# One hand-written order of opening steps replaced by another in a fused mLSTM and feed-forward kernel

## The chip, the cores and the metric

The kernel runs on one core of a Trainium2 chip. The metric is the device time of one execution in microseconds (us), the median of several runs.

## The reference

Eight heads and four batches of a gated linear recurrence over 768 tokens (mLSTM), whose output, 3072 tokens of 320 channels, goes through a two-matrix feed-forward with a leaky rectifier.

```python
for t in range(S):                      # q, k, v: (4, 8, 768, 40)
    m_new = maximum(f_gate[:, :, t] + m, i_gate[:, :, t])
    f_stab, i_stab = exp(f_gate[:, :, t] + m - m_new), exp(i_gate[:, :, t] - m_new)
    C = f_stab * C + i_stab * outer(v_t, k_t)
    n = f_stab * n + i_stab * k_t
    y[:, :, t] = sigmoid(o_gate[:, :, t]) * (C @ q_t) / maximum(abs(n @ q_t), 1.0)
x = y as (3072, 320)
h = x @ w_in                            # w_in: (320, 2048)
g = maximum(h, 0) + alpha * minimum(h, 0)
out = g @ w_out                         # w_out: (2048, 320)
```

## The kernel before, in words

The 768 tokens of a batch are cut into 6 chunks of 128, so there are 24 chunks; two chunks make a group of 256 tokens, of which there are 12. A chunk is worked out in parallel form: scores of q and k (tile pS) are multiplied with decays (tile E), and that is multiplied with the values (pH); a running state C carries what came before, and its part is pI. The result xn is gated (og), transposed (p1, p2), split into a high and a low part (XH, XL), and then goes through the feed-forward: eight "up" products a group (ph), a rectifier (g), a split into gh and gl, and eight "down" products (po). Because all products are made of high and low parts, each weight is split too: the raw words are loaded (wi, wr, wo), a copy t is made by ScalarE (`scale`), the lowest bits are joined to it by VectorE (`join`), ScalarE casts it to the high part (`high`: WH, W, OH), and the low part (`low`: WL, W, OL) is the difference of the two, on VectorE, or on GpSimd where the step's name ends in p or P instead of l or L. Where a weight's step x is replaced by y, ScalarE's preparation of the lowest bits (`three`, L865) is left out and VectorE does a shift more (`shift`, L871) before the join (L879 instead of L877).

Nothing is scheduled by a planner when the kernel is built. The table ORDER names some 400 steps of the opening (the first batch's six chunks, the splitting of the weights, and the first two groups' feed-forward), and each name is one call; after it PATTERN repeats for the later groups. The program `pin`s that order: on each engine instructions run in the order in which the steps stand, and waits for other engines' results are added. All loads but two are issued by SyncE (SP) in the same order, so a load whose buffer is still read holds back all loads behind it.

Names of steps that matter below: `kfz` clears the two buffers kf (four memsets on GpSimd, L311 and L312), `li0` is GpSimd's subtraction that the first biases need (g_li, L1215), `bj0` is VectorE's that reads it (L1218). `wd` scales the keys (kd, L172), on GpSimd if the chunk's number is in KDP. `um` and `uc` make the next state: if the chunk is in CP, the decayed old state is one GpSimd instruction of 104 partitions (the multiply at L210), else two on VectorE (L221, one for each parity of the heads); VectorE then adds the new product (L222). `gx` is the multiply that writes xn, on GpSimd if the chunk is in XNP. A feed-forward up product has five steps: with U, R, S, G, K the low part gl is on VectorE, with V, r, s, g, N it is on GpSimd (L785). `psa` hands out the four PSUM banks of one pool, two with tag a and two with tag b, in turns.

Of the kernel before, what the change touches and what calls it, by code (L numbers as in the profile page):

```python
# [17 lines left out]
def kernel(ctx: ExitStack, tc: tile.TileContext, q, k, v, i_gate, f_gate, o_gate, w_in, w_out, alpha, out):  # L18
# [19 lines left out]
    ps_o = ctx.enter_context(tc.tile_pool(name="ps_o", bufs=1, space=bass.MemoryType.PSUM))  # L38
    ps_a = ctx.enter_context(tc.tile_pool(name="ps_a", bufs=2, space=bass.MemoryType.PSUM))
    turns = ["b", "a"]  # L40

    def psa(name, tag=None):
        if tag is None:
            turns.reverse()
            tag = turns[0]
        return ps_a.tile([P, 512], F32, tag=tag, name=name)
# [61 lines left out]
    def by_token_of(n, j):  # L108

        t = (qn_t, kn_t)[j][n % NQ]  # L110
        if n < NDIR:
            return t[:, :, :D]
        return t.rearrange("p h e -> p (h e)")[:, : H * D].rearrange("p (h e) -> p h e", e=D)
# [54 lines left out]
    def weighed(n):  # L168

        b, c = divmod(n, NC)  # L170
        kd = sb.tile([P, H, D], F32, tag="kd", name=f"kd{n}")
        (nc.gpsimd if n in KDP else nc.vector).tensor_tensor(  # L172
            kd, by_token_of(n, 1), wT[:, c, b * H : (b + 1) * H].unsqueeze(2).broadcast_to([P, H, D]), ALU.mult
# [8 lines left out]
    def update_steps(n):  # L182
# [8 lines left out]
        if not late or j == 0 or n - 1 not in pus:  # L191
            pu = psa(f"pu{n}", kept(n, "a", NDIR + 1))
            if late and j == 0:
                pus[n] = pu
        else:
            pu = pus.pop(n - 1)
# [11 lines left out]
        old, new = C_t[(n - 1) % 3], C_t[n % 3]  # L208
        if c > 0 and n in CP:
            nc.gpsimd.tensor_tensor(  # L210
                new[:R], old[:R], gamB[:R, b * H : (b + 1) * H, c : c + 1].broadcast_to([R, H, VA]), ALU.mult
            )
        for par in range(2):
# [4 lines left out]
            else:  # L218
                if n not in CP:
                    gam = gamB[r, b * H + par : (b + 1) * H : 2, c : c + 1].broadcast_to([D, NPR, VA])  # L220
# [111 lines left out]
    def values(n, E):  # L332

        pH = psa(f"pH{n}")
        va = va_t[n // GC % NV][:, n % GC]
        for h in range(H):
            nc.tensor.matmul(
                repeated(pH, h * VA, VA), E[h % 2][:, h // 2 * P : (h // 2 + 1) * P],
                va[:, h].unsqueeze(1).broadcast_to([P, WIDE // VA, VA]), start=True, stop=True,
            )  # L340
        return pH[:, : H * VA].rearrange("p (h e) -> p h e", e=VA)
# [27 lines left out]
    def values_by_parts(n, Es):  # L369

        V = vbs.pop(n)
        S = sb.tile([P, H, VA], F32, tag="T", name=f"S{n}")
        for par in range(2):
            pH = psa(f"pH{n}_{par}", kept(n, "a", NDIR))
            for p in range(NPR):
                for k, e in enumerate(Es[par]):
                    nc.tensor.matmul(  # L377
                        pH[:, p * 3 * VA : (p * 3 + 3 - k) * VA], e[:, p * P : (p + 1) * P],
                        V[:, 2 * p + par, : 3 - k], start=k == 0, stop=k == 2,
                    )  # L380
            yield
            nc.vector.tensor_reduce(
                by_parity(S, par), pH[:, : NPR * 3 * VA].rearrange("p (r k e) -> p r e k", k=3, e=VA),
                mybir.AxisListType.X, ALU.add,
            )
            yield S
# [29 lines left out]
    def gated_steps(n, hv):  # L416
# [23 lines left out]
        else:  # L440
            nc.gpsimd.tensor_tensor(sg, sg, rb, ALU.mult)
        yield
        (nc.gpsimd if c > 0 and n in XNP else nc.vector).tensor_tensor(
            xn[:, :DM].rearrange("p (h d) -> p h d", d=D), hv[:, :, :D], sg, ALU.mult
# [211 lines left out]
    def first_stacks():  # L656
# [20 lines left out]
    NBF = 6  # L677
    GF = NDIR // GC
    BEHIND = 4
    XNP = range(2, NBF)  # L680
    KDP = range(1, 24)
    CP = range(6, 24)
    OBA = range(0)
    WIDE = 3 * VA
    ORDER = """warm18 kfz alT lf0z warm2 warm2 i00d i00s sca0 lf0a lf0b dq0 L0 sp01 qT0 dq1 alC li0 bj0 wt0 bTt kT0 i00x qc0 kc0 ewj
        i01d sca1 bTc ex01 sp00 sc00 qT1 wTt eeL wTc qc1 wd0 li1 lf1a lf1b kT1 sc01 i00j ex00 kc1 eTt Cz eTc sp11 ex11
        dv0 wg01 i01s wd1 L1 um0 uc0 i01x lpa um1 sp10 wg00 gma gmd ex10 i01j i00h fm1 ft1 sc11 do0 sc10 wg10 bj1 wtl
        blt ewl blc i00p o0d o0s r0d o0x gmm gmc r0s r0x v0 wg11 lpb lpc lpd uc1 dq2 qT2 o2d gr0 wlt og1 warm2 wlc r0j
        i11d lpe o0j i01h i01p gg0 qc2 dq3 gx0 gp0 kT2 v1 eel elt elc sp21 kc2 sc21 dL r0H ta1 gr1 gg1 sp20 ex21 qT3
        wg21 i10d dv1 r0h gx1 gp1 r0p r0L ex20 wd2 sc20 wg20 qc3 x0 x1 xa0 xd0 dq4 fm2 wd3 xa1 xd1 i10s F0 ft2 o2s o2y  # L690
        sp31 o0h ex31 kT3 o2j o2h i10y i10j um2 U00 o0l V01 kc3 R00 i11s uc2 i11y i11j o2l do1 i10h i10l sp30 r01 qT4
        qc4 ex30 S00 v2 sc31 i20d i20s ta2 gr2 i20x wg31 o1d og2 gg2 gx2 kT4 i20j kc4 sc30 wg30 G00 K00 i21d fm3 ft3
        s01 i20h o1s i20p i11h i11p o1x r2d o1j i21s i21x sc41 v3 um3 i21j uc3 ta3 dL4 U02 V03 r2s r2y o3d gr3 sc40
        ex41 fm4 R02 dq5 o1h o1l o4d g01 r2j N01 qT5 i21h i21p o3s S02 o3x G02 K02 dL5 wg41 i31d ft4 D00 wd4 dq6 o3j
        qc5 dv2 r2h r2p r03 ex40 o4s r2H D01 o4x gg3 s03 o3h o4j gx3 o5d gp3 wg40 i30d V04 r04 s04 dv3 o4h V05 gp2 x2
        x3 xa2 xd2 o6d do2 wd6 kT5 g04 r2P g03 o3l xa3 r05 o4l s05 v4 xd3 kc5 i31s ta4 N03 N04 i31y i31j i30s o5s o5x
        F1 V10 gr4 r10 um4 uc4 dL6 i30x um6 U11 ex50 R11 o5j s10 uc6 S11 ex51 g10 i31h dL7 i31p sc50 N10 i30j dq7 wg50
        U12 fm5 ft5 o5h sc51 wg51 v5 o7d R12 S12 ta5 D10 G11 K11 o6s o6x gr5 og3 gg5 G12 gx5 gg4 D11 K12 D12 i30h i30l
        gx4 U13 gp5 D02 tp0 do3 U06 o7s gp4 o5l o6j vp0 R13 tp1 g05 S13 G13 N05 K13 o7x o6h D13 vp1 o7j U07 tp2 tp3
        R06 S06 R07 x4 x5 xa5 xd5 D03 D04 D05 S07 o7h o7l G06 K06 o6l D06 xa4 xd4 G07 K07 D07 Z0"""  # L700
    PATTERN = """og.-1 ua.0 uA.1 m1.0 V4<< tf.1 ub.0 vb.1 xn.-1 xp.-1 V5<< tg.1 g2<< m0.0 N2<< vc.1 c1.0 r4<< vb.0 d1.0 th.1 h1.0 ti.1 xw.-1 uc.0
        s4<< ud.0 D2<< ue.0 U6<< g4<< l1.0 g3<< N3<< uf.0 r5<< c0.0 vd.1 vc.0 ua.1 sh.1 X:-1 lG.-1 lG.2 ub.1 s5<< N4<<
        R6<< d0.0 g5<< ug.0 h0.0 l0.0 uc.1 V7<< N5<< vd.0 D3<< D4<< D5<< S6<< ta.2 tb.2 xa:-1 uh.0 lL.2
# [8 lines left out]
    def in_full():  # L712

        names = ORDER.split()
        done = set(names)
# [651 lines left out]
```

## Time and profile before

| what | value |
|---|---|
| median of 3 runs | 465.33 us (464.62 to 466.82) |
| the profiled execution, its own time | 465.35 us |
| its span, first to last instruction | 463.6 us |
| TensorE busy | 452.8 us, 98% |
| VectorE, ScalarE, GpSimd busy | 329.8, 315.0, 308.4 us |

The profiled execution is as long as the median run. Its time is 1.75 us over its span, which lies around the instructions. The engines are called PE (TensorE), DVE (VectorE), ACT (ScalarE), POOL (GpSimd) and SP in the rows; PEld is TensorE's loading of weights. TensorE's granted clock was full in all of the stretches shown.

### The profile page before, as it was taken

Reading aid. Unit: us, or ns where it says so; the run is one execution under the profiler, and the core shown is the slowest. Engines: PE = TensorE matmul, PEld = TensorE weight load, DVE = VectorE, ACT = ScalarE, POOL = GpSimd, SP = SyncE. Lnnn points to the kernel's source line nnn. Section 1 sums busy time; section 2 is a strip of 40 time slices with the busy share of each in tenths; the row PEclk is TensorE's granted clock in tenths of the full one; section 3 lists DMA queues with packets and bytes.
Section 4 is the critical chain, followed back from the end, with each engine's and each line's share of the span. In section 5 each row is a group of like instructions: output and inputs, shape, how many; then the busy total and the mean of one; then the engine's idle time right before and its main releaser. Section 6 shows DMA issues by size and latency. Waiting matters only on the chain.

```text
span 463.6 us, 11813 instructions
## 1 busy us (share of the span) xinstructions
PE 452.8 (98%) x4366; PEld 442.0 (95%) x4366; DVE 329.8 (71%) x692; ACT 315.0 (68%) x707; POOL 308.4 (67%) x377
## 2 busy tenths in 40 slices
PE   8989989999999999999999999999999999999996
PEld 6879978999999999999999999999999999999996
DVE  4989998747776787886875887886776786764321
ACT  4899898676857858758856958757857858423331
POOL 8551674854698697588888598588888686324231
PEclk9999999999999999999999999999999999999999
DMA  9999994869775775888997686688796463020000
GB/s 184 177 221 252 277 252 118 175 122 190 151 182 147 138 184 160 137 174 173 158 187 176 122 197 168 133 166 180 153 206 156 107 154 90 1 84 15 28 2 28
DMA packets 186306, 68.67 MB, mean 148 GB/s; under 512 B 150234, under 2 KB 178506, under 8 KB 186250
## 3 DMA queue, kind: packets, MB, share of 16 engines
q1 hardware_dynamic: 186170, 67.83, 67.2%
q8 instruction: 34, 0.56, 0.5%
q14 instruction: 22, 0.18, 0.2%
q10 hardware_dynamic: 80, 0.11, 0.1%
HBM read 40.44 MB, written 7.57 MB: 104 GB/s over the span
## 4 chain that ended last, share of the span: by engine, by line
PE 83%; DVE 5%; DMA 5%; SPq 3%; ACT 3%; issue 1%; ACTq 0%; DVEq 0%
PE po L796 36%; PE ph L759 5%; PE ph L765 5%; PE ph L762 5%; PE ph L760 5%; PE ph L761 5%; PE ph L764 4%; PE ph L763 4%; PE ph L766 4%; PE pH L377 4%; PE pS L515 4%; DMA wi<-in_moe_w_in_dram 2%; DMA wr<-in_moe_w_in_dram 2%; PE pI L403 1%; PE pu L203 1%; DMA qn<-in_q_dram 1%
## 5 line engine op out<-in xcount | busy, mean ns | idle before, releaser
L785 POOL TENSOR_TENSOR gl<-g,gh 128x512 fp32r<-128x512 f32 x77 | 100.5, 1306 | 42.9 <-ACT gh L783 39.6
L796 PE MATMUL po<-OH,gh 128*128 128x320 f32 x368 | 110.7, 312 | 0.0
L796 PE MATMUL po<-OL,gh 128*128 128x320 f32 x368 | 109.3, 309 | 0.0
L769 ACT ACTIVATE g<-ph 128x512 f32<-128x512 f32 x96 | 57.1, 596 | 58.2 <-PE ph L766 56.0
L774 DVE SCALAR_TENSOR_TENSOR g<-g,oma,ph 128x256 f32<-128x256 f32 x156 | 66.8, 469 | 32.7 <-ACT g L769 32.3
L796 PEld LDWEIGHTS po<-OL,gh 128*128 128x128 f32 x368 | 69.2, 188 | 0.1
L796 PEld LDWEIGHTS po<-OH,gh 128*128 128x128 f32 x368 | 69.1, 188 | 0.0
L796 PE MATMUL po<-OH,gl 128*128 128x320 f32 x368 | 69.0, 309 | 0.0
L759 PE MATMUL ph<-XH,WH 128*128 128x256 f32 x192 | 57.2, 298 | 1.1 <-ACT wo L865 0.7
L796 PEld LDWEIGHTS po<-OH,gl 128*128 128x128 f32 x368 | 57.9, 188 | 0.0
L764 PE MATMUL ph<-XL,WH 128*128 128x256 f32 x192 | 54.3, 283 | 0.9 <-DVE XL L623 0.9
L765 PE MATMUL ph<-XL,WH 128*128 128x256 f32 x192 | 54.3, 283 | 0.0
L762 PE MATMUL ph<-XH,WL 128*128 128x256 f32 x192 | 54.3, 283 | 0.0
L760 PE MATMUL ph<-XH,WH 128*128 128x256 f32 x192 | 54.1, 282 | 0.0
L761 PE MATMUL ph<-XH,WL 128*128 128x256 f32 x192 | 54.1, 282 | 0.0
L364 ACT CAST E<-pS 128x512 bf16<-128x512 f32 x72 | 41.6, 582 | 18.0 <-DVE pS L361 14.0
L763 PE MATMUL ph<-XH,W 128*128 128x256 f32 x192 | 53.4, 278 | 0.2 <-POOL W L891 0.2
L766 PE MATMUL ph<-XL,W 128*128 128x256 f32 x192 | 53.4, 278 | 0.0
L783 ACT CAST gh<-g 128x512 fp32r<-128x512 f32 x77 | 46.5, 618 | 9.1 <-DVE g L774 6.6
L486 ACT ACTIVATE E<-Lb,bT 128x128 f32<-128x128 f32 x160 | 50.0, 392 | 0.0
L361 DVE TENSOR_TENSOR pS<-pS,E 128x512 f32<-128x512 f32 x36 | 24.8, 690 | 29.6 <-PE pS L515 26.2
L759 PEld LDWEIGHTS ph<-XH,WH 128*128 128x128 f32 x192 | 36.1, 188 | 2.0 <-ACT wo L865 0.9
(197 smaller groups left out, 1123.2 us busy)
## 6 DMA issues: line engine op xcount, KB each, us to landing
Lb<-L_d SPq DMA_DIRECT2D x20, 512.0 KB
wo<-in_moe_w_out_dram SPq DMA_DIRECT2D x8, 640.0 KB
wi<-in_moe_w_in_dram SPq DMA_DIRECT2D x8, 512.0 KB
qn<-in_q_dram SPq DMA_DIRECT2D x24, 160.0 KB
kn<-in_k_dram SPq DMA_DIRECT2D x24, 160.0 KB
va<-in_v_dram SPq DMA_DIRECT2D x24, 160.0 KB
og<-in_o_gate_dram SPq DMA_DIRECT2D x24, 160.0 KB
out_dram<-ob SPq DMA_DIRECT2D x11, 320.0 KB
```

Of the source, the lines that this page charges most:

```text
L759: nc.tensor.matmul(dst, WH[half][:, 0, hs], XH[:, 0], start=True, stop=False)
L760: nc.tensor.matmul(dst, WH[half][:, 1, hs], XH[:, 1], start=False, stop=False)
L761: nc.tensor.matmul(dst, WL[half][:, 0, hs], XH[:, 0], start=False, stop=False)
L762: nc.tensor.matmul(dst, WL[half][:, 1, hs], XH[:, 1], start=False, stop=False)
L763: nc.tensor.matmul(dst, W2[:, fs], X2, start=False, stop=False)
L764: nc.tensor.matmul(dst, WH[half][:, 0, hs], XL[:, 0], start=False, stop=False)
L765: nc.tensor.matmul(dst, WH[half][:, 1, hs], XL[:, 1], start=False, stop=False)
L766: nc.tensor.matmul(dst, W2[:, fs], X2L, start=False, stop=True)
L769: nc.scalar.activation(gt, ph, AF.Relu, scale=-1.0)
L774: nc.vector.scalar_tensor_tensor(out=y[:, e], in0=gt[:, e], scalar=oma[:, f : f + 1], in1=ph[:, e], op0=ALU.mult, op1=ALU.add)
L785: (nc.vector if split else nc.gpsimd).tensor_tensor(gl, y, gh.bitcast(F32), ALU.subtract)
L796: nc.tensor.matmul(po[j], x[:, e, j * P : (j + 1) * P], W[f // NB][:, f % NB], **ends)
```

## The change

The same steps stand in another order. Some change their kind: eight low parts of weights change engine, seven of them from VectorE to GpSimd (o0, o1, o2, o4, o7 and i10 from l to p, and one half of a remainder, r0L to r0P), and one the other way (i00p to i00l); two weights take the step y in place of x (i01, o4); one up product takes the VectorE form (V04 to U04). Three sets of chunks change: keys of chunk 4 go to VectorE (chunk 5 ends the batch and has none), the decayed states of chunks 1 to 4 go to GpSimd, and xn of chunk 1 goes to GpSimd and that of chunk 4 to VectorE. The first 51 PSUM banks that `psa` hands out follow a written list of tags instead of taking turns. The count of warming products stays at 24. PATTERN is unchanged.

```diff
     turns = ["b", "a"]
+    first_turns = list("abababaababaababababaababaababababaabbaabbaabaaabaa")
 
     def psa(name, tag=None):
+        if tag is None and first_turns:
+            tag = first_turns.pop(0)
         if tag is None:
...
-    XNP = range(2, NBF)
-    KDP = range(1, 24)
-    CP = range(6, 24)
+    XNP = (1, 2, 3, 5)
+    KDP = (1, 2, 3, *range(6, 24))
+    CP = (1, 2, 3, 4, *range(6, 24))
...
-    ORDER = """warm18 kfz alT lf0z warm2 warm2 i00d i00s sca0 lf0a lf0b dq0 L0 sp01 qT0 dq1 alC li0 bj0 wt0 bTt kT0 i00x qc0 kc0 ewj
+    ORDER = """sca0 i00d dq0 warm18 lf0a i01d alT li0 i00s i00x lf0b warm3 dq1 lf0z warm2 kfz dv0 L0 bj0 sp01 qT0 alC bTt
```

First place, GpSimd's queue at the start of the program. Before, from the last small memset on (g_li is the subtraction of `li0`, kf the buffers of `kfz`):

```order
L1002 MEMSET unit 32x1
L311 MEMSET kf_133 40x512
L312 MEMSET kf_133 64x512
L311 MEMSET kf_134 40x512
L312 MEMSET kf_134 64x512
L1215 TENSOR_TENSOR g_li<-g_WH_96,g_WL_97 32x256
L1014 TENSOR_TENSOR g_WL_97<-g_WH_96,g_L 32x256
```

After (all lines of the changed file are three to four lines further down):

```order
L1006 MEMSET unit 32x1
L1219 TENSOR_TENSOR g_li<-g_WH_96,g_WL_97 32x256
L314 MEMSET kf_133 40x512
L315 MEMSET kf_133 64x512
L314 MEMSET kf_134 40x512
L315 MEMSET kf_134 64x512
L1018 TENSOR_TENSOR g_WL_97<-g_WH_96,g_L 32x256
```

The subtraction moved ahead of the four memsets.

Second place, VectorE's queue around the third chunk's state (C_87) and the first low parts of the out weights (OL). Before:

```order
L879 SCALAR_TENSOR_TENSOR t_wi_0_538<-wi_0_487,t_wi_0_538 128x512
L891 TENSOR_TENSOR OL_105<-t_wo_362,OH_104 128x640
L221 TENSOR_TENSOR C_87<-C_86,gamB 40x4x42
L222 TENSOR_TENSOR C_87<-C_87,pu_568 40x4x42
L221 TENSOR_TENSOR C_87<-C_86,gamB 40x4x42
L222 TENSOR_TENSOR C_87<-C_87,pu_568 40x4x42
L871 TENSOR_SCALAR t_wi_1_616<-t_wi_1_616 128x512
L879 SCALAR_TENSOR_TENSOR t_wi_1_616<-wi_1_415,t_wi_1_616 128x512
L891 TENSOR_TENSOR OL_564<-t_wo_542,OH_563 128x640
L891 TENSOR_TENSOR WL_103<-t_wi_0_538,WH_102 128x512
```

After:

```order
L883 SCALAR_TENSOR_TENSOR t_wi_0_579<-wi_0_473,t_wi_0_579 128x512
L411 TENSOR_TENSOR T_609<-pI_541,eT 128x336
L225 TENSOR_TENSOR C_87<-C_87,pu_590 40x4x42 x2
L778 SCALAR_TENSOR_TENSOR ph_0_562<-g_0_581,oma,ph_0_562 128x256 x2
L1238 TENSOR_TENSOR T_609<-T_609,pH_600 128x336
L875 TENSOR_SCALAR t_wi_1_611<-t_wi_1_611 128x512
```

Two low parts of 128x640, one of 128x512 and both multiplies with gamB left VectorE's queue there.

Third place, GpSimd's queue from the third chunk's keys on (kd). Before:

```order
L891 TENSOR_TENSOR W_73<-t_wr_371,W_73 64x512
L172 TENSOR_TENSOR kd_501<-kn_77,wT 128x320
L172 TENSOR_TENSOR kd_532<-kn_78,wT 128x320
L443 TENSOR_TENSOR xn_670<-T_540,og_341 128x320
L891 TENSOR_TENSOR WL_711<-t_wi_0_667,WH_710 128x512
L891 TENSOR_TENSOR WL_103<-t_wi_1_616,WH_102 128x512
```

After:

```order
L175 TENSOR_TENSOR kd_445<-kn_77,wT 128x320
L453 COPY xn_389<-xn_389 128x64
L895 TENSOR_TENSOR WL_103<-t_wi_1_320,WH_102 128x512
L446 TENSOR_TENSOR xn_456<-T_341,og_327 128x320
L453 COPY xn_456<-xn_456 128x64
L175 TENSOR_TENSOR kd_502<-kn_78,wT 128x320
L895 TENSOR_TENSOR W_73<-t_wr_397,W_73 64x512 x2
L895 TENSOR_TENSOR OL_105<-t_wo_345,OH_104 128x640
L213 TENSOR_TENSOR C_87<-C_86,gamB 104x336
L895 TENSOR_TENSOR OL_584<-t_wo_504,OH_583 128x640
L895 TENSOR_TENSOR WL_103<-t_wi_0_579,WH_102 128x512
```

The third chunk's keys stand ahead of a weight's low part and of the remainder's (W) now, and both low parts OL, the second half of W and the state's multiply were added.

## Rows read from the trace of the kernel before

**Rows 1.** Stretches: length, busy us (instructions) by engine, TensorE's clock, DMA share, GB/s.

```profile
0.00:12.00 12.00, 9.76 (x66) 7.59 (x66) 4.82 (x14) 6.19 (x13) 10.39 (x28) 1.00 1.02 183
12.00:46.00 34.00, 31.89 (x306) 28.91 (x305) 31.28 (x65) 30.85 (x75) 13.34 (x17) 1.00 0.97 218
46.00:78.50 32.50, 29.60 (x273) 28.17 (x273) 29.00 (x57) 28.17 (x60) 19.82 (x21) 1.00 0.85 213
78.50:460.00 381.50, 381.50 (x3724) 377.36 (x3724) 264.70 (x557) 249.41 (x562) 264.89 (x314) 1.00 0.63 136
```

**Rows 2.** TensorE's waits, 0 to 80 us: us in total, times, longest.

```profile
PE ph L764 <- DVE XL L623: 0.9, 1, 0.9
PE pb L100 <- DVE xn L443: 0.8, 1, 0.8
PE pH L337 <- DVE E L1101: 0.8, 2, 0.6
PE ph L759 <- ACT wo L865: 0.7, 1, 0.7
PE ps_gw L1022 <- ACT E L1080: 0.5, 1, 0.5
PE ph L759 <- DVE g L774: 0.4, 1, 0.4
...
PEld pH L337 <- DVE E L1101: 1.2, 2, 0.8
```

**Rows 3.** The chain that ended last, 46 to 80 us: start, us, what.

```profile
60.39 0.80 ACT wo L865
...
69.17 0.69 DVE t_wi L879
...
71.54 0.83 DVE t_wo L877
```

**Rows 4.** Timeline, 25.8 to 29.2 us, GpSimd and VectorE.

```profile
25.86 1.26 POOL L891 TENSOR_TENSOR WL<-t_wi,WH 128x512 fp32r<-128x512 f32 x1 [0.55 <-ACT WH L887]
25.92 1.55 DVE L439 SCALAR_TENSOR_TENSOR og<-og,r 128x320 f32<-128x320 f32 x1
...
29.09 0.49 DVE L439 SCALAR_TENSOR_TENSOR og<-og,r 128x320 f32<-128x320 f32 x1
```

**Rows 5.** VectorE's groups, 0 to 80 us: busy us, mean ns, idle before.

```profile
L877 DVE SCALAR_TENSOR_TENSOR t_wo<-t_wo,wo 128x640 uint32<-128x640 uint32 x5 | 5.7, 1140 | 0.4 <-ACT wo L865 0.2 <-POOL xn L443 0.2
L877 DVE SCALAR_TENSOR_TENSOR t_wi<-t_wi,wi 128x512 uint32<-128x512 uint32 x5 | 4.6, 923 | 0.0
L891 DVE TENSOR_TENSOR OL<-t_wo,OH 128x640 fp32r<-128x640 f32 x5 | 4.0, 810 | 0.0
L439 DVE SCALAR_TENSOR_TENSOR og<-og,r 128x320 f32<-128x320 f32 x4 | 3.4, 861 | 0.0
L221 DVE TENSOR_TENSOR C<-C,gamB 40x168 f32<-40x168 f32 x8 | 2.5, 318 | 0.1
L879 DVE SCALAR_TENSOR_TENSOR t_wr<-wr,t_wr 128x512 uint32<-128x512 uint32 x1 | 1.8, 1769 | 0.0
L871 DVE TENSOR_SCALAR t_wo<-t_wo 128x640 uint32<-128x640 uint32 x1 | 0.5, 494 | 0.4 <-ACT t_wo L855 0.4
```

**Rows 6.** GpSimd's groups, 0 to 80 us, and C over the whole span.

```profile
L891 POOL TENSOR_TENSOR W<-t_wr,W 64x512 fp32r<-64x512 f32 x3 | 3.8, 1277 | 1.0 <-ACT W L887 0.8
L172 POOL TENSOR_TENSOR kd<-kn,wT 128x320 f32<-128x320 f32 x5 | 3.5, 719 | 0.1
...
L230 POOL TENSOR_TENSOR C<-C,gamB 40x336 f32<-40x336 f32 x12 | 9.0, 753 | 0.0
```

**Rows 7.** SyncE's longest wait total, 0 to 80 us, and the stretch around it.

```profile
SPq L106 <- POOL kd L172: 7.4, 2, 4.1
...
32.00:36.00 4.00, 3.67 (x43) 3.18 (x44) 3.33 (x8) 3.61 (x10) 2.71 (x4) 1.00 0.37 55
```

**Rows 8.** Timeline of the start, VectorE.

```profile
6.68 0.41 DVE L1218 TENSOR_TENSOR g_WH<-g_li,g_L 32x256 f32<-32x256 f32 x1 [0.42 <-POOL g_li L1215]
```

More of the change, by code (lines that the diff above doesn't have):

```diff
@@ L679 @@
     BEHIND = 4
-    XNP = range(2, NBF)
-    KDP = range(1, 24)
-    CP = range(6, 24)
+    XNP = (1, 2, 3, 5)
+    KDP = (1, 2, 3, *range(6, 24))
+    CP = (1, 2, 3, 4, *range(6, 24))
     OBA = range(0)
     WIDE = 3 * VA
-    ORDER = """warm18 kfz alT lf0z warm2 warm2 i00d i00s sca0 lf0a lf0b dq0 L0 sp01 qT0 dq1 alC li0 bj0 wt0 bTt kT0 i00x qc0 kc0 ewj
[L686 to L700, printed above, removed]
@@ new lines @@
+    ORDER = """sca0 i00d dq0 warm18 lf0a i01d alT li0 i00s i00x lf0b warm3 dq1 lf0z warm2 kfz dv0 L0 bj0 sp01 qT0 alC bTt
+        bTc qc0 wt0 ewj kT0 kc0 sp00 wTt ex01 sc00 sca1 i00j wTc wd0 qT1 Cz li1 sp11 kT1 sc01 eeL ex00 wg00 lf1a
+        wg01 eTt qc1 lf1b kc1 L1 eTc um0 uc0 sc11 ex11 wd1 sp10 fm1 sc10 i01s i01y lpa o0d do0 gma gmd i00h ex10
+        i01j ft1 bj1 wtl o0s og1 warm1 ewl um1 wg11 wg10 i00l lpb blt gmm gmc o0x r0d dq2 v0 lpc lpd blc gr0 uc1 r0s
+        r0x eel i01h i11d o2d wlt wlc dq3 lpe gg0 kT2 r0j gx0 qT2 v1 qc2 sp21 wd2 kc2 ta1 elt gp0 gr1 i01p dL sp20
+        elc r0H dv1 o0j i10d r0h dq4 sc21 qT3 gg1 gx1 ex21 wg21 gp1 ex20 wd3 o2s qc3 sc20 wg20 x0 x1 xa0 kT3 r0P r0p
+        i20d xd0 xa1 xd1 fm2 sp31 kc3 F0 o0h o2y o2j ex31 U00 i10s R00 o2h i10y i10j do1 um2 o0p v2 ft2 i11s sp30
+        uc2 i10h o2p V01 S00 o1d i20s qT4 ta2 dL4 i11y kT4 sc31 gr2 ex30 i20x i11j fm3 qc4 i21d r2d i20j dq5 i10p
+        og2 kc4 i11h o1s wg31 ft3 i20h sc30 gg2 i11p wg30 G00 K00 gx2 r01 s01 i20p wd4 o1x sc41 i21s i21x o1j i21j
+        v3 ta3 um3 uc3 U02 gr3 ex41 R02 V03 D00 sc40 r2s r2y fm4 S02 o1h o1p r03 g01 r2j o3d i21h o3s N01 i21p G02
+        o3x r2h r2p o4d dv2 i31d K02 dq6 qT5 dL5 o3j ft4 ex40 o5d r2H D01 dv3 s03 o4s U04 i30d do2 wg41 o4y qc5 R04
+        gg3 kT5 V05 o3h kc5 gp2 gx3 wg40 o4j S04 gp3 x2 x3 wd6 o3l r05 xa2 G04 o4h v4 xd2 xa3 r2P g03 o4p i31s N03
+        K04 xd3 s05 ta4 i31y gr4 o5s o5x i31j F1 V10 um4 uc4 ex51 r10 o6d ex50 um6 U11 R11 i30s dL6 uc6 sc51 sc50
+        s10 o5j i30x i31h g10 wg51 U12 dL7 wg50 S11 fm5 N10 i31p i30j G11 ft5 o7d R12 v5 S12 ta5 o5h D10 i30h og3
+        dq7 K11 gr5 gg5 G12 K12 o6s D11 gg4 gx5 o6x D12 U13 tp0 i30l gx4 D02 o6j R13 vp0 o5l g05 do3 o7s gp5 S13 U06
+        N05 G13 gp4 o7x K13 o6h D13 tp1 U07 o7j tp2 R06 x4 R07 x5 tp3 S06 vp1 D03 xa5 xd5 xa4 o6l D04 G06 S07 o7h
+        D05 K06 G07 o7p D06 xd4 K07 D07 Z0"""
```

## The prediction

> **What bounds the kernel now.** I read the stretches first [rows 1]. From 78.5 us to 460 us TensorE is busy in every microsecond (381.50 of 381.50), so nothing that VectorE, ScalarE, GpSimd or a load does there can shorten it, and the diff leaves that part's order alone. Only the opening, up to 78.5 us, has room: TensorE is idle there for 12.00 - 9.76 = 2.24, 34.00 - 31.89 = 2.11 and 32.50 - 29.60 = 2.90 us, 7.25 us in all. Some of this is the program's start and can't go. A microsecond taken out of the opening should be a microsecond of the end, since the dense part only slides forward.
>
> Second, TensorE's waits in the opening [rows 2]. Four of them end with VectorE: 0.9 for the low part XL, 0.8 for xn (the next product wants the bank that xn still reads), 0.8 for the decayed scores E, 0.4 for the rectified g; 2.9 us together. ScalarE ends 0.7 and 0.5. Matmul ends are modelled, so the true waits are somewhat longer: for E the weight loads show 1.2 where the matmuls show 0.8.
>
> Third, the chain of waits [rows 3] and what VectorE does on it. VectorE is busy for 29.00 of the 32.50 us before 78.5 us, ScalarE for 28.17, GpSimd for 19.82 [rows 1]; from 12 to 46 us it is 31.28, 30.85 and 13.34 of 34. VectorE and ScalarE are nearly full, GpSimd has 34.00 - 13.34 + 32.50 - 19.82 = 33.3 us free.
>
> Fourth, whether VectorE's instructions cost what they should. At 25.92 us the multiply of og takes 1.55 us; at 29.09 us the same takes 0.49 [rows 4]. During the first GpSimd makes a weight's low part, from 25.86 us for 1.26 us; the difference, 1.06 us, is about what was left of that when og came up (1.20). The group's means say the same of others [rows 5]: og 861 ns over four, the joins of t_wo 1140 against 0.83 us alone and of t_wi 923 against 0.69 alone [rows 3], that of t_wr 1769 against 0.69 for the same size. So blocked time on VectorE up to 80 us is 4 x 0.37 + 5 x 0.31 + 5 x 0.23 + 1.08 = 5.3 us.
>
> The Trainium skill ("SBUF — State Buffer", Who interferes with whom) gives the rule: a VectorE instruction with two SBUF inputs contends with a GpSimd instruction that reads SBUF, and the loser waits for the whole of the other; one with a PSUM input doesn't. The rows above agree for og. By the rule alone moving work to GpSimd makes more blockers, which is the rival "lock" below, priced there from rows.
>
> **The change part by part.** *Taken from VectorE* ahead of the last wait (at 78 us): four low parts of 128x640 at 0.81 (3.24), half a remainder, in width like a join without a block (0.69), eight multiplies of C at 0.318 (2.54) [rows 5]; i10 and i00 swap. That is 6.5 us. *Given to VectorE:* one keys' product, which I price like og unblocked, the same size (0.49) [rows 4], one low part gl of 128x512 (0.69, as t_wi alone [rows 3]), two shifts (0.49 and at most 0.49) [rows 5]: 2.2 us. Net -4.3 us. xn of chunk 1 and of chunk 4 change places: nothing.
>
> *Given to GpSimd* [rows 6]: half a remainder 1.28; four low parts of 128x640, which no row has on GpSimd. Between 1.28 (width doesn't count) and 1.28 x 640/512 = 1.60 I take 1.60, since its time follows the row's length (320 long 0.72, 512 long 1.28): 6.4. Four C multiplies of 104 partitions: 0.75 by the row of 40 partitions, 1.95 if partitions counted; I take 0.75, because the remainder's 64 partitions cost 1.28 as do 128 in [rows 4]: 3.0. Taken off it: keys 0.72, one gl 1.28. Net +8.7 us, into 33.3 us free. If the upper price held for C, +13.5, which still fits.
>
> *Taken from ScalarE:* two preparations of lowest bits, at 0.80 for 128x640 [rows 3] and at most that for 128x512: 1.5 us at most.
>
> *SyncE's queue.* SyncE waited 7.4 us for keys, in two waits [rows 7]: the loads of the next chunk's k may not overwrite kn until kd has read it, and every load issued later stood behind. After the first of them the DMA engines were busy only 0.37 of 32 to 36 us, 2.5 us of lost transfer time. In the new GpSimd queue the third chunk's keys stand ahead of a weight's and the remainder's low parts, so that wait should nearly go. TensorE's shown waits for loads are small, so I count it at nothing here; if the loads set the pace it is worth up to 2.5 us (a rival).
>
> *The start.* bj0 waited 0.42 us for li0 [rows 8], which stood behind four memsets in GpSimd's queue; now it stands ahead, so the first biases come 0.4 us earlier. The memsets end later, but the first scores that need kf come several products after.
>
> *Other moves* (warming products, PSUM tags, the places of loads) I count at nothing: the shown wait for a bank is the 0.5 behind ScalarE [rows 2], so they may give back 0.5 or take about as much.
>
> *Sum.* VectorE loses 4.3 us of work and, if the order keeps its two-input instructions clear of GpSimd's, part of 5.3 us of blocking. I take half of that, 2.6, so 6.9 us less on a queue that had 6.2 us idle in 66.5 (12 to 78.5 us). That is more than the 2.9 us of TensorE's waits on it, so I let all four go: 2.9, plus 0.9 for the modelled ends (0.2 to 0.4 each, as the E row shows), plus 0.4 at the start: 4.2. With VectorE out of the way ScalarE, as full as it, will end waits that don't show now: I give back a quarter, 1.0 (chosen; the trace bounds it between nothing and all). Net -3.2 us against the profiled execution's 465.35, which lies at the median: **462.1 us**. Bounds: all idle but the first 2.24 gone and 1.4 for modelled ends, 465.35 - 6.4 = 458.9; everything given back and nothing won, 465.4.
>
> **The rivals.** *ScalarE sets the pace.* It is busy for 30.85 of 34 and 28.17 of 32.5 us [rows 1], and the change takes at most 1.5 us from it; the waits behind ScalarE stay and VectorE's turn into waits for casts. Then the gain is 1.5: 463.9 us. For it: the two engines are equal within 0.9 us in both stretches. Against: four of the six larger waits end with VectorE.
>
> *Loads set the pace.* DMA share is 0.97 in the middle stretch. If TensorE's pace there follows the loads, only the gap at 32 to 36 us is won, 2.5 us: 462.9 us. Against: no long wait of TensorE ends with a load.
>
> *The lock, slower.* GpSimd's reading of SBUF grows by 8.7 us, a quarter of the 33.2 us it was busy from 12 to 78.5 us. VectorE's instructions with two SBUF inputs ahead of the last wait fall from 49 to 35 (counted in the two orders). At the same chance of meeting, blocking would be 5.3 x 35/49 x 1.26 = 4.8 us, so VectorE still gains 4.8. It decides where each of the 35 waits over (5.3 + 4.3)/35 = 0.27 us on average, against 0.11 now. The new low parts of 1.60 us could do that: if every second of the 35 met one and waited half of it, blocking would be 14 us, VectorE 4.4 us later, and TensorE, which would wait for it in full, ends at 469.7 us. Against: the order was moved around on both engines at once and the meetings can be placed; for: a meeting hangs on a few tenths of a microsecond, and ScalarE's and the loads' times shift them.
>
> **How the numbers follow.** Chances: forecast 0.45, loads 0.13, ScalarE 0.28, lock 0.14. Half a per cent, 2.3 us, is about what a measurement of this kernel can tell from no change, so faster means under 463.0. The forecast's spread (459 to 463.5) and the loads make 0.58 faster; ScalarE's case and the edges of the forecast 0.28 same, with what is left of the lock's milder end; slower 0.14. The range goes from the bound of the full gain, 458.9, to 466.0, past ScalarE's case and the mild end of the lock.
>
> **What would show it.** Right: og, t_wo, t_wi and t_wr nearer to their unblocked times in the opening, VectorE's busy time up to the last wait down by 6 us or so, the rows "ph behind XL", "pH behind E" and "pb behind xn" gone or halved, GpSimd fuller by 9 us, the last idle of TensorE at about 75 us and from there an unchanged dense part of 381.5 us. SyncE's long wait for kd shorter, with no gap at 32 to 36 us. Wrong: the same sum of TensorE idle with ScalarE or GpSimd named as releaser, or VectorE instructions with two SBUF inputs at 1.5 us and more behind low parts of 128x640, or new idle in the dense part, should the later groups' loads or parts come late for a TensorE that arrives earlier.

## The result and the profile after

The changed kernel takes 461.02 us (median of 4 runs, 460.83 to 461.09) where the kernel before took 464.98 (median of 4, 464.43 to 466.82): a ratio of 0.9911, 95% interval 0.9892 to 0.9931, 4.0 us less. The profiled execution took 460.83 us, its span is 459.1 us (463.6 before).

The stretches of the changed kernel (columns as in [rows 1]; the last row is the stretch of [rows 7]):

```profile
0.00:12.00 12.00, 10.09 (x69) 8.08 (x70) 7.12 (x17) 6.34 (x15) 9.59 (x30) 1.00 0.94 183
12.00:46.00 34.00, 32.82 (x313) 29.92 (x313) 28.33 (x56) 31.30 (x73) 22.75 (x22) 1.00 1.09 238
46.00:74.00 28.00, 27.54 (x263) 26.63 (x262) 26.20 (x52) 25.55 (x56) 21.94 (x21) 1.00 0.86 221
74.00:455.50 381.50, 381.46 (x3725) 377.33 (x3725) 259.56 (x559) 249.85 (x563) 265.17 (x314) 1.00 0.63 136
...
32.00:36.00 4.00, 3.34 (x39) 2.72 (x37) 3.10 (x5) 3.66 (x9) 3.85 (x4) 1.00 0.97 216
```

The opening now ends at 74 us and not at 78.5, which is 4.5 us earlier; the two profiled executions are 465.35 - 460.83 = 4.5 us apart too, 0.5 more than the medians. TensorE's idle time in it is 1.91 + 1.18 + 0.46 = 3.55 us instead of 7.25, so 3.7 of the 4.5 us are idle time that went; the rest, 0.8, is shorter busy time. This split belongs to the one trace: in the trace of *changed_again*, the same kernel (below), the opening ends at 74.6 us with 3.06 us of idle time, so idle time there is 4.2 us less and busy time 0.3 more. The dense part is as long as it was, 381.46 of 381.50. VectorE's busy time up to the dense part fell from 65.1 us [rows 1] to 7.12 + 28.33 + 26.20 = 61.65; GpSimd's rose from 43.55 to 54.28.

TensorE's waits, 0 to 80 us (columns as in [rows 2]):

```profile
PE ph L767 <- POOL W L895: 0.8, 2, 0.6
PE pb L1056 <- DVE g_L L1157: 0.5, 1, 0.5
PE pqk L269 <- DVE C L225: 0.5, 1, 0.5
```

All six waits of [rows 2] are gone, those on ScalarE too. What is listed now beside the wait for the program's first constants is 1.8 us in three rows, one of them behind GpSimd. The row for g_L is missing in the trace of *changed_again*; the other two stand there as well.

VectorE's groups of the changed kernel, 0 to 80 us (columns as in [rows 5]; its line numbers are three or four higher):

```profile
L881 DVE SCALAR_TENSOR_TENSOR t_wo<-t_wo,wo 128x640 uint32<-128x640 uint32 x4 | 4.5, 1129 | 0.1
...
L883 DVE SCALAR_TENSOR_TENSOR t_wi<-wi,t_wi 128x512 uint32<-128x512 uint32 x4 | 3.1, 771 | 0.0
...
L442 DVE SCALAR_TENSOR_TENSOR og<-og,r 128x320 f32<-128x320 f32 x6 | 3.0, 507 | 0.1
L883 DVE SCALAR_TENSOR_TENSOR t_wo<-wo,t_wo 128x640 uint32<-128x640 uint32 x2 | 2.8, 1419 | 0.0
```

GpSimd's groups of the same stretch:

```profile
L895 POOL TENSOR_TENSOR OL<-t_wo,OH 128x640 fp32r<-128x640 f32 x4 | 7.1, 1772 | 1.9 <-ACT OH L891 1.1 <-DVE gl L789 0.6
L895 POOL TENSOR_TENSOR W<-t_wr,W 64x512 fp32r<-64x512 f32 x4 | 6.6, 1643 | 0.3
L213 POOL TENSOR_TENSOR C<-C,gamB 104x336 f32<-104x336 f32 x4 | 3.7, 923 | 2.1 <-DVE gamB L1194 2.1
```

og, 861 ns in [rows 5], is at 507, nearly unblocked. The joins of t_wo are not: 1129 after 1140, and 1419 for the two that follow a shift. GpSimd's own instructions became longer too: W 1643 on average after 1277 [rows 6].

To have one number for this I add up, from the timelines up to 80 us, how much VectorE's joins, low parts, og and keys (24 to 29 instructions, as records are missing) took over their shortest durations: 0.68 us for 512 columns, 0.82 for 640, 0.48 for 320. That is **5.4 us before and 4.5 after**; the shifts, over 0.42 us (0.49 for 640), add 0.5 before and 1.8 after. Together 5.9 and 6.3. I call it blocked time below, as "joins and so on + shifts".

### The profile page after: what moved, and what is told of

It is laid out like the page before. It is cut to its first block, busy times and chain, and to the rows that moved or that the text cites. A ratio compares the mean times of both kernels' runs of the same rounds, so it can differ in the third digit from the quotient of the medians.

```text
span 459.1 us, 11805 instructions
## 1 busy us (share of the span) xinstructions
PE 452.4 (99%) x4366; PEld 442.2 (96%) x4366; DVE 321.2 (70%) x682; ACT 313.5 (68%) x705; POOL 319.4 (70%) x385
## 4 chain that ended last, share of the span: by engine, by line
PE 91%; DMA 2%; ACT 2%; POOL 2%; DVE 2%; issue 1%; DVEq 0%; ACTq 0%; POOLq 0%
PE po L800 36%; PE ph L763 6%; PE ph L769 5%; PE ph L766 5%; PE ph L768 5%; PE ph L764 5%; PE ph L765 5%; PE ph L767 5%; PE ph L770 5%; PE pH L380 4%; PE pS L518 4%; PE pu L206 2%; PE pS L1101 1%; DMA wo<-in_moe_w_out_dram 1%; PE pI L406 1%; PE pH L340 1%
## 5 line engine op out<-in xcount | busy, mean ns | idle before, releaser
L789 POOL TENSOR_TENSOR gl<-g,gh 128x512 fp32r<-128x512 f32 x76 | 98.6, 1299 | 40.0 <-ACT gh L787 36.9
L767 PEld LDWEIGHTS ph<-XH,W 128*128 128x128 f32 x192 | 36.7, 191 | 1.2 <-POOL W L895 1.2
```

The source lines that it names most:

```text
L767: nc.tensor.matmul(dst, W2[:, fs], X2, start=False, stop=False)
L789: (nc.vector if split else nc.gpsimd).tensor_tensor(gl, y, gh.bitcast(F32), ALU.subtract)
```

## The experiments

Each was timed against the kernel before on the same chip (medians 464.99, 464.49 and 464.84 in three sessions), so kernels of different sessions are compared by their ratios; 0.1% is 0.46 us.

### The order by itself, the engines by themselves

*order_alone*: the new order and list of banks, with each step's old form and the old sets.

```diff
-    XNP = (1, 2, 3, 5)
-    KDP = (1, 2, 3, *range(6, 24))
-    CP = (1, 2, 3, 4, *range(6, 24))
+    XNP = range(2, NBF)
+    KDP = range(1, 24)
+    CP = range(6, 24)
...
-    i01y i00l r0P o0p o2p i10p o1p o4y U04 R04 S04 G04 o4p K04 o7p
+    i01x i00p r0L o0l o2l i10l o1l o4x V04 r04 s04 g04 o4l N04 o7l
```

> The new order and the list of bank tags, but every step on the engine and in the form that it had before (low parts, keys, states, xn, the two joins, the fifth up product). If the moved work is what counts (VectorE has its 4.3 us back, in an order that left no room for it), most of the 4.0 us is lost: 463.5 to 465.5 us. If the order alone made the gain, 461.7 us or less. VectorE's busy time up to TensorE's last wait should be some 4 us above that of the changed kernel in the first case.

*engines_alone*: the reverse, the old order without the list, with the new forms in their old places and the new sets.

> The old order, with the new engines and forms. If the moved work is what counts, 462 to 463.5 us: VectorE is 4.3 us shorter and its four waits shrink. If the order made the gain, no change or worse, 464.5 to 466.5 us, since low parts of 1.6 us on GpSimd meet VectorE's instructions with two SBUF inputs where the old order put them.

Measured: order_alone 467.18 us, ratio 1.0043 (1.0028 to 1.0057); engines_alone 465.78, 1.0016 (1.0005 to 1.0027). Neither half gives anything; each by itself costs, 2.2 and 0.8 us, and both together give 4.0. order_alone came out above both of the ranges that I had expected. In it TensorE's longer waits end with VectorE, but for one behind GpSimd's W (its waits up to 80 us):

```profile
PE pS L1100 <- DVE C L225: 1.5, 1, 1.5
...
PE pb L103 <- DVE XL L626: 1.3, 1, 1.3
PE ph L766 <- POOL W L894: 1.1, 1, 1.1
PE pS L1100 <- DVE T L1237: 1.0, 1, 1.0
PE pqk L269 <- DVE C L225: 1.0, 1, 1.0
```

GpSimd waits for work, and this is its longest wait there:

```profile
POOL WL L894 <- ACT WH L890: 14.9, 1, 14.9
```

I read it so: the order is made for a VectorE that doesn't do the moved work. With that work on VectorE its busy time up to the dense part (which begins at 80.5 us here) is 65.00 us, 3.4 more than the changed kernel's 61.65; GpSimd stands 14.9 us at one low part, and states (C), XL and T come late. SyncE's wait for kd [rows 7] has no row here, and the DMA engines are 0.89 and 1.04 busy in the two halves of 32 to 36 us, so this kernel has the loads' gap closed and is slower all the same.

In engines_alone three of TensorE's four waits for VectorE stay (up to 80 us; the one for XL is gone), that for g is three times as long as in [rows 2], and two behind ScalarE have come, for kf and E (L1080):

```profile
PE ph L759 <- ACT kf L323: 1.2, 1, 1.2
PE ph L759 <- DVE g L774: 1.2, 1, 1.2
PE pb L100 <- DVE xn L443: 0.9, 1, 0.9
PE pH L337 <- DVE E L1101: 0.8, 2, 0.6
PE pqk L266 <- ACT E L1080: 0.8, 1, 0.8
```

Its timeline from 35 to 43 us shows where VectorE's time went; GpSimd's rows, then VectorE's:

```profile
35.54 2.15 POOL L891 TENSOR_TENSOR OL<-t_wo,OH 128x640 fp32r<-128x640 f32 x1 [0.49 <-ACT OH L887]
37.66 0.94 POOL L210 TENSOR_TENSOR C<-C,gamB 104x336 f32<-104x336 f32 x1
38.56 1.55 POOL L891 TENSOR_TENSOR OL<-t_wo,OH 128x640 fp32r<-128x640 f32 x1
...
36.18 1.80 DVE L871 TENSOR_SCALAR t_wi<-t_wi 128x512 uint32<-128x512 uint32 x1
38.01 2.65 DVE L879 SCALAR_TENSOR_TENSOR t_wi<-wi,t_wi 128x512 uint32<-128x512 uint32 x1
```

A shift of 0.42 us takes 1.80, a join of 0.68 takes 2.65, and they end 0.3 and 0.55 us after one of GpSimd's 128x640 subtractions has ended (at 37.69 and 40.11). The join had come up 0.55 us before the second of these began, during GpSimd's multiply of C, and stood until both were over. Blocked time is 9.4 + 2.5 us against 5.4 + 0.5 before: 6.0 us more, over the 4.3 us of work that left VectorE. This is the rival "lock" of the prediction, in the old order.

### Is it GpSimd's reading?

In both orders GpSimd's low parts of weights read only 8 columns (16 for OL) and fill the time with two memsets, which write SBUF and read none of it; beyond those columns the low parts are left zero. In the old order a low part takes GpSimd as long as in engines_alone: WL 2 x 0.516 + 0.248 = 1.28 us (1.32 there), OL 2 x 0.641 + 0.495 = 1.78 (1.70). In the new order, where GpSimd had been held up itself, it is shorter than in the changed kernel: OL 1.55 us (1.77), W 1.51 (1.64).

```diff
-            (engine or nc.vector).tensor_tensor(l, t, h.bitcast(F32), ALU.subtract)
+            if engine is None:
+                nc.vector.tensor_tensor(l, t, h.bitcast(F32), ALU.subtract)
+                return
+            engine.tensor_tensor(l[..., :8], t[..., :8], h[..., :8].bitcast(F32), ALU.subtract)
+            for _ in range(2):
+                engine.memset(l[..., 8:].bitcast(F32), 0.0)
```

> The kernel of engines_alone, where GpSimd's low parts of weights read only 8 columns and then fill the rest by two memsets each, so that GpSimd works for as long but hardly reads SBUF (the low parts themselves are left out: those are zero). If the lock on reading is what ate the gain of the moved work (10.4 us of VectorE's time over its unblocked times there), VectorE's blocked time should fall below 5 us and the time to 462 to 463.5 us. If the lock isn't the cause, within 0.7 us of engines_alone, 465.8.

> The changed kernel with the same replacement. It has 6.0 us of blocked time on VectorE, but TensorE's waits are short: if the new order has put the blocked time where it doesn't count, 460.3 to 461.0 us; if blocked time still counts in full, 458.5 us.

Measured: in the old order 462.14 us, ratio 0.9944 (0.9932 to 0.9957), against 1.0016 for engines_alone: 0.72%, 3.3 us. In the new order 459.33, 0.9885 (0.9870 to 0.9901), against 0.9911: 0.26%, 1.2 us, between the two cases expected. Blocked time fell from 9.4 + 2.5 to 1.1 + 2.1 us in the old order and from 4.5 + 1.8 to 2.5 + 1.2 in the new. The old order's timeline, GpSimd and then VectorE:

```profile
35.10 1.46 POOL L896 MEMSET OL<- 128x624 f32 x2
...
39.04 1.09 POOL L896 MEMSET WL<- 128x504 f32 x2
...
35.00 1.00 DVE L871 TENSOR_SCALAR t_wi<-t_wi 128x512 uint32<-128x512 uint32 x1
36.03 0.69 DVE L879 SCALAR_TENSOR_TENSOR t_wi<-wi,t_wi 128x512 uint32<-128x512 uint32 x1
...
39.07 0.69 DVE L879 SCALAR_TENSOR_TENSOR t_wi<-wi,t_wi 128x512 uint32<-128x512 uint32 x1
```

The join at 39.07 us runs wholly beside memsets and takes its 0.69. In the old order TensorE's waits for g and E shrink with it (0.5 and 0.6 us, after 1.2 and 0.8) and those for xn and for ScalarE's E go; that for kf stays at 1.2. So GpSimd's reads, at equal length of its work, hold VectorE up, and in the old order this decides whether the moved work pays. The 1.2 us of the new order are less certain: the two intervals overlap, GpSimd's low parts became shorter as well, and TensorE's wait for W (0.8 us) went. The Trainium skill ("SBUF — State Buffer", Who interferes with whom) says that two SBUF inputs on VectorE contend with a GpSimd instruction that reads SBUF and not with one that only writes; the joins agree. The shift at 35.00 us, one input, took 1.00 beside a memset, and the next one, at 38.23 us, 0.81; the same section lists tensor_scalar among the operations that can take the pair of ports shared with GpSimd, and these two times fit that.

The reads are not all: with them gone in both, the new order is still better by 0.9944 - 0.9885 = 0.59%, 2.7 us. With them its advantage is 1.0016 - 0.9911 = 1.05%, 4.9 us.

### Does VectorE's work count in the new order?

In the changed kernel one thing each goes back: *lows_back* all eight low parts of weights, *states_back* the states of chunks 1 to 4, *half_back* one half of the remainder.

```diff
 lows_back
-    r0P o0p o1p o2p o4p o7p i10p i00l
+    r0L o0l o1l o2l o4l o7l i10l i00p
 states_back
-    CP = (1, 2, 3, 4, *range(6, 24))
+    CP = range(6, 24)
 half_back
-    r0P
+    r0L
```

> The changed kernel with all eight low parts of weights on the engines that they had before (r0, o0, o1, o2, o4, o7, i10 on VectorE again, i00 on GpSimd), nothing else. If VectorE's work is what counts, about 4.0 us more on it and 463 to 465 us. If the order had room for it, 461.5 us or less.

> The changed kernel with the decayed states of chunks 1 to 4 on VectorE again (eight multiplies of 0.32 us), nothing else. If VectorE's work is what counts, 2.5 us more on it, in short pieces: 462 to 463.5 us. If not, 461.3 us or less.

> The changed kernel with one low part, the first half of the first remainder (W, 64x512), on VectorE again. In the changed kernel TensorE's longest wait ends with it on GpSimd (0.6 us, up to 0.8 with the weight load). If that wait counts, 460.2 to 460.6 us against 461.0. If VectorE's work counts there, 0.7 us more of it cancels that or worse: 461.0 to 461.7 us.

Measured: lows_back 463.88 us, ratio 0.9986 (0.9977 to 0.9995), 0.75% or 3.5 us over the change; states_back 462.87, 0.9960 (0.9947 to 0.9972), 2.3 us over it; half_back 462.63, 0.9951 (0.9939 to 0.9963), 1.8 us over the change in its own session (0.9912, *changed_again* below), which is more than I had expected in either case. So in this order each of these pieces costs time when it goes back to VectorE. The costs are not shares of the gain: lows_back and states_back add up to 5.8 us, and the change gave 4.0. TensorE's waits up to 80 us that came with it, in lows_back first, where the longer one ends with ScalarE (why it was late there was not traced):

```profile
PE ph L762 <- ACT t_wi L858: 1.4, 1, 1.4
PE pb L103 <- DVE XL L626: 0.7, 1, 0.7
```

In states_back:

```profile
PE pqk L269 <- DVE C L225: 1.0, 1, 1.0
...
PE pS L1101 <- DVE T L1238: 0.7, 1, 0.7
```

In half_back:

```profile
PE pb L103 <- DVE XL L626: 2.0, 1, 2.0
```

half_back is the clearest: one instruction of 0.69 us makes TensorE wait 2.0 us. Its timeline, GpSimd's row and then VectorE's:

```profile
31.32 1.26 POOL L894 TENSOR_TENSOR W<-t_wr,W 64x512 fp32r<-64x512 f32 x1
...
31.39 1.74 DVE L894 TENSOR_TENSOR W<-t_wr,W 64x512 fp32r<-64x512 f32 x1
33.16 0.42 DVE L626 TENSOR_TENSOR XL<-p,XH 128x256 fp32r<-128x256 f32 x1
```

The same place in the changed kernel:

```profile
30.94 2.96 POOL L895 TENSOR_TENSOR W<-t_wr,W 64x512 fp32r<-64x512 f32 x2
...
30.89 0.42 DVE L626 TENSOR_TENSOR XL<-p,XH 128x256 fp32r<-128x256 f32 x1
```

On VectorE the half starts 0.07 us after GpSimd's half of the same remainder, waits for it, takes 1.74 us, and XL, which stands behind it, comes at 33.16 instead of 30.89. On GpSimd the two halves run one behind the other beside XL, which has an input in PSUM. After its wait of 2.0 us TensorE worked at its lower clock, 1.2 GHz, for some 3 us in the profiled execution (463.35 us, the slowest of six); the granted clock is the third figure from the end:

```profile
34.50:37.90 3.40, 3.39 (x18) 3.12 (x19) 1.54 (x4) 3.14 (x8) 1.78 (x2) 0.55 1.03 202
```

In half_back_clears_first, below, the same wait of 2.0 us was not followed by a lower clock, and the profiled execution took 462.19. The six executions of half_back fall into two groups by the mean granted clock of the whole program: 462.06, 462.07 and 462.09 us at 0.999 to 1.000, and 463.17, 463.27 and 463.35 at 0.996. So at full clock the half costs 462.07 - 460.93 = 1.1 us against *changed_again*, the executions with the lower clock are 1.2 us longer still, and the 1.8 of the medians lies between the two groups. The profiled execution of lows_back (465.20 us) has such a stretch too, 0.69 from 20 to 24 us, and lies 1.3 us over its median. Ahead of that stretch TensorE had no wait over 0.51 us (from 8 us on), so what lowered the clock is not shown.

### The start, and the loads

*clears_first* puts the memsets `kfz` back ahead of `li0`; *half_back_clears_first* does that and half_back's edit; *keys_late* moves the third chunk's keys, `wd2`, 14 steps later.

```diff
 clears_first
-    sca0 i00d dq0 warm18 lf0a i01d alT li0 i00s i00x lf0b warm3 dq1 lf0z warm2 kfz dv0 L0 bj0
+    sca0 i00d dq0 warm18 lf0a i01d alT kfz li0 i00s i00x lf0b warm3 dq1 lf0z warm2 dv0 L0 bj0
 keys_late
-    qc2 sp21 wd2 kc2 ta1 elt gp0 gr1 i01p dL sp20 elc r0H dv1 o0j i10d r0h dq4
+    qc2 sp21 kc2 ta1 elt gp0 gr1 i01p dL sp20 elc r0H dv1 o0j i10d r0h wd2 dq4
```

> The changed kernel with the four clearing memsets of kf ahead of li0 again. If the start is worth what the prediction counted, 0.3 to 0.5 us more, 461.4 us. If the first biases have slack in the new order, no difference, 461.0 us.

> Both half_back and clears_first. If the two waits are separate and both count, 460.0 us or a little less; if the W half is needed where it is, 460.7 us or more.

> The changed kernel with the third chunk's keys (kd) issued 14 steps later, just ahead of the load that they hold back. If loads set the pace (the rival), SyncE's queue waits again and 1.5 to 2.5 us are lost, 462.5 to 463.5 us. If loads have slack, within 0.5 us of 461.0.

Measured: clears_first 460.64 us, ratio 0.9906 (0.9889 to 0.9922); half_back_clears_first 462.23, 0.9947 (0.9935 to 0.9959); keys_late 461.50, 0.9919 (0.9904 to 0.9934). The intervals of the first and the last hold the change's 0.9911: neither edit can be told from nothing. The start of the changed kernel, GpSimd's row and VectorE's in the timeline:

```profile
4.51 0.86 POOL L1219 TENSOR_TENSOR g_li<-g_WH,g_WL 32x256 f32<-32x256 f32 x1 [0.73 <-DVE g_WL L1148]
...
4.91 0.74 DVE L1154 TENSOR_TENSOR g_lf<-g_lf,g_WL 32x255 f32<-32x255 f32 x1
...
6.54 0.41 DVE L1222 TENSOR_TENSOR g_WH<-g_li,g_L 32x256 f32<-32x256 f32 x1
```

The start of clears_first:

```profile
4.95 0.52 POOL L314 MEMSET kf<- 40x512 f32 x1
...
5.14 0.41 DVE L1153 TENSOR_TENSOR g_lf<-g_lf,g_WL 32x255 f32<-32x255 f32 x1
...
6.80 0.41 DVE L1221 TENSOR_TENSOR g_WH<-g_li,g_L 32x256 f32<-32x256 f32 x1 [0.47 <-POOL g_li L1218]
```

`li0` reads SBUF beside VectorE's two-input subtraction, which takes 0.74 us for 0.41; the memset in the same place holds nobody up. The last bias subtraction, `bj0`, came only 6.68 - 6.54 = 0.14 us earlier than before [rows 8], and 0.09 of that is the first load, which landed earlier: from VectorE's first scan, at 3.84 us before and 3.75 in the changed kernel, `bj0` stands at 2.84 and 2.79 us. TensorE's 0.5 us for g_L above is not shown to be the other side of it. In clears_first that row is gone, but it is gone in *changed_again* too, where the subtraction takes 0.74 us as well.

In keys_late the third chunk's keys start at 27.2 us instead of 24.0, the DMA engines' share from 32 to 34 us is 0.72 instead of 1.00, and the median is 0.5 us above the change. The long wait for kd did not come back, so this run alone bounds the loads weakly; order_alone, where the gap is closed and the time is longer, and writes_only_old_order, where SyncE waits 4.4 and 1.4 us for keys, the DMA engines' share from 32 to 34 us is 0.54, and 462.14 is reached, bound them better.

### The change again

*changed_again* is the changed kernel with an empty line.

> The changed kernel once more, beside these two on the same chip. All theories: 461.0 us; it shows what a repetition differs by, 0.3 us or less.

Measured: 460.93 us, ratio 0.9912 (0.9899 to 0.9925).

Not tried: the list of PSUM banks apart from the order, since in that form the new order can't run without it. What the list is worth is open. The other moved pieces (the keys, xn, the two forms y, the up product) were not put back one by one either.

## Why the prediction was right, and where it wasn't

The time, 461.02, lies 1.1 us under the 462.1 predicted, inside the forecast's own spread.

**Right: where the gain is.** Only the opening got shorter, by idle time of TensorE, and the dense part slid forward. The four waits behind VectorE (2.9 us) went, and 0.5 to 1.0 us of others behind it came. That putting work back on VectorE costs there is shown: 0.69 us of it cost 1.1 us at full clock, all low parts 3.5, the states 2.3.

**Right: VectorE's work, 4.3 us less.** Measured 65.1 - 61.65 = 3.45 less busy, with blocked time 0.4 up: 3.9 us of work. The 6 us or so that I expected of the busy time counted blocking that stayed.

**Wrong: "I take half of that, 2.6".** The blocked time didn't halve. It went from 5.9 to 6.3 us with the shifts, which I hadn't counted as blockable; joins and so on alone gave back 0.9. What the order did was to keep the moved work from doubling it, as it does in the old order (11.9), and to place it where TensorE doesn't wait. I read the sum as having held because 3.9 us less work was enough for waits of 2.9. The amount of blocked time alone doesn't set the time: lows_back, added up the same way, has less of it than the changed kernel (4.0 + 0.9 us) and is 3.5 us slower.

**Wrong: "plus 0.4 at the start".** It was 0.14 us at `bj0`, 0.05 without the earlier load: the moved subtraction met VectorE's own, which took 0.74 us for 0.41. Nothing was won there, and clears_first, with the old place, is as fast.

**Mis-sized: "I give back a quarter, 1.0".** Nothing came back from ScalarE, though its busy time from 12 to 46 us is 31.30 of 34. What was given back is 0.8 us behind GpSimd's W and 1.0 behind VectorE (g_L, in one trace of two, and C), while both waits behind ScalarE (1.2 us) went, which the forecast had left standing. So of the 4.1 us in [rows 2] 2.3 net went, and of the 3.7 us idle won 1.4 lies in waits too short for the list, against the 0.9 that I had for modelled ends.

**Luck in the total.** The forecast's 2.9 + 0.9 + 0.4 - 1.0 = 3.2 us stands against 4.1 of waits gone, 1.8 come, 1.4 of short waits and 0.8 of busy time, 4.5 between the two profiled executions. The start and the halved blocking didn't come, ScalarE took nothing back, and its own two waits went; that these errors nearly cancel is luck.

**GpSimd.** C of 104 partitions costs 0.76 us at the shortest, as priced (0.75), so partitions didn't count here. OL of 128x640 costs 1.55 unblocked in engines_alone, against 1.60; I take the rest of its mean of 1.77 for blocking. GpSimd's busy time rose by 10.7 us, 2.0 more than the 8.7 predicted; W alone is 4 x 0.37 = 1.5 us longer than by [rows 6]. It had the room.

**The rivals.** ScalarE did not set the pace. SyncE's wait for kd went and the gap at 32 to 36 us closed (0.97 after 0.37), as foreseen, and that is worth little, as argued above. The lock was the nearest: its point of decision is 5.3 + 4.3 = 9.6 us of blocking of two-input instructions. engines_alone came up to it with 9.4, and past it with the shifts (11.9, against 5.9 + 4.3 = 10.2), and is 0.8 us slower than before. In the changed kernel it did not come true: the same moved work has 6.3 us of blocking there.

**Open.** The 2.7 us by which the new order is better without GpSimd's reads are not traced to single moves. Of the changed kernel's time 1.2 us go when GpSimd's low parts don't read, at the edge of what the intervals can tell, and no version here that computes everything got that; clears_first, 460.64, is not measurably better.

## What to carry to other kernels

Before moving work from VectorE to GpSimd, count the VectorE instructions with two SBUF inputs that will run beside it: here 4.3 us of moved work brought 6.0 us of blocking until the order changed as well. An order and an assignment of engines belong together, so try them together: each alone was slower, both were faster by 0.9%. A wait is best read on the instruction behind it: 0.69 us put ahead of XL made TensorE wait 2.0 us, since it came 0.07 us after GpSimd's half had begun and took 1.74. And a median over executions with different clocks mixes two things, so look at the clock of each execution: here 1.1 us was the half and 1.2 us went with the clock.

## What the runs showed of the hardware that was not expected

A shift with one SBUF input is held up as well: 1.80 us for 0.42 beside GpSimd's 128x640 subtraction, and 1.00 and 0.81 beside memsets, which do not hold up a join (0.69). GpSimd is held up too: W 1643 ns on average against 1277 before. A wait of 2.0 us of TensorE was followed by its lower clock (0.55 granted) for about 3 us in one profiled execution and not in another; in lows_back the clock fell to 0.69 from 20 to 24 us with no wait over 0.51 us ahead of it.
